# Attention with two expert layers on one core: a reordered opening, later casts, and weight decodes at other places

## The chip, the core and the metric

The kernel runs on one core of a Trainium2 chip. Its engines work from instruction queues of their own: TensorE (PE, matmuls, with its weight loads as PEld), VectorE (DVE), ScalarE (ACT), GpSimd (POOL) and SyncE (SP, which issues the DMAs here). The time is device microseconds of one execution, and the median of several is compared.

## What is computed

Attention over 2 batches of 8 heads with 768 positions of 64 numbers. Each query and each key is assigned to the nearest of 16 centroids of its head, and a query sees only keys of its own cluster. Two expert layers follow: the first with a leaky activation, the second behind an RMS norm with a SiLU gate.

```python
q_assign = argmax(einsum('bhsd,hcd->bhsc', q_n, c_n))      # q_n, k_n, c_n: unit vectors
k_assign = argmax(einsum('bhsd,hcd->bhsc', k_n, c_n))
scores = where(q_assign[..., None] == k_assign[..., None, :], q @ k.T / 8, -1e9)
attn = exp(scores - max(scores));  attn = attn / (sum(attn) + 1e-9)
x = reshape(attn @ v)                                      # 1536 tokens x 512
h = x @ w_in;  x = (max(h, 0) + alpha * min(h, 0)) @ w_out # 512 -> 2048 -> 512
xn = x / sqrt(mean(x * x) + 1e-6) * rms_g
out = (silu(xn @ w_gate) * (xn @ w_val)) @ w_out           # 512 -> 1536 -> 512
```

The expert weights arrive as 64-bit floats.

## The kernel before

**Attention** handles the 16 heads of both batches as 8 pairs. A pair has two phases of 384 queries, a phase has 6 slots, and a slot is one tile of 128 keys for both heads: `st_tile` multiplies it (L549 and L550 for each head), and ScalarE takes the exponential (L551). After every second slot `pv_tiles` multiplies with the values (L565) and sums the weights (L570). So there are 96 slots.

Each number of q and k is split in a high part, which is rounded (`prep_hi`, a ScalarE cast, L466, into a `stage` buffer), and a low part, the remainder (`prep_lo`, a subtraction on GpSimd, L471). Two operands per head, `op1` and `op2`, are put together from `stage` by DMAs that SP issues: `prep_dma_a` (L475, one copy) and `prep_dma_b` (L482 to L484, three). The clusters go into `op1` as 16 rows of one-hot code, built on chip and written by `prep_dma_oh` (L488), so that the mask falls out of the same matmul. The row maximum comes from `max_tile` a few slots ahead (two matmuls, L507, and one reduction over 768 columns on VectorE, L511); it is split (L516, L517) and turned into two rows of `op2` (`max_rows`, L534, L536).

The clusters of a pair need the vectors' norms. `prep_sq` squares on ScalarE (L367), `prep_ss` sums (L378: a tree on GpSimd for the pairs in `ASIDE`, 1 to 3), and `rnorm` makes three Newton steps (`prep_norm`; on VectorE L332 to L334, for `ASIDE` pairs on GpSimd L326 to L329). Then `prep_sims` multiplies with the centroids and transposes (L397, L402, L407), `prep_scale` scales (L414), `prep_arg` finds the nearest centroid (L423 to L436), and `prep_oht` turns the code round (L445, L446).

Three things set the order. `setup` writes the opening (pair 0 and the start of pair 1) by the letters of `CHAIN`, each of which takes the next step of one list: s and t sum squares of pairs 0 and 1, n Newton, l the loads of pair 1, m similarities, a scale and argmax, d the `prep_dma_a` copies, p the pattern (L294), o one-hot, q the squares of pair 1, w matmuls on zeros (L313) in the numbers of `WARM`. From then on `plan` places each step by (slot, order within the slot), from the tables `FIRST`, `SECOND`, `THIRD`, `FOURTH`, `FIFTH` and `PAIR` for pairs 0, 1, 2, 3, 4 and the rest, counted from the pair's first slot, and the maximum tiles from `AHEAD`. The inputs of a pair come into `nat` (for the norms) and `raw` (for the casts), two buffers of one name that each next pair takes over.

**The expert layers** (`Moe`) run 8 groups of the first layer and 6 of the second, each over three blocks of 512 tokens. `up` makes two halves of 128 hidden columns, and `down` two halves that are added into `x` (`down_mm`, then `down_add`, L914 on VectorE). Every product is three matmuls (`mm3`, L812): high by high, low by high, high by low. A group's weight halves are decoded on chip, one half a time: four instructions on VectorE (L788, L790, L793, L794), a ScalarE cast to the high part (L801), and two on GpSimd for the low part (L798, L799; on VectorE for those in `EAGER`). `plan` of `Moe` writes `up`, `down` and `decode_next` in a row: decodes go behind any half step with an open weight half, unless it is in `calm`. The RMS norm of a block is `rms_sq`, `rms_sum` (L933 to L942) and `rms_mul` (L950 to L958).

Of the kernel before, what the change touches and what calls it, by code (L numbers as in the profile page):

```python
# [47 lines left out]
FIFTH = {  # L48
    **PAIR,
    "load": ((-37, 6.1), (-37, 6.2), (-35, 1.8), (-35, 1.9)),  # L50
    "hi": ((-30, 4), (-29, 4)),
    "lo": ((-29, 4.5), (-28, 4.5)),
}
# [638 lines left out]
class Moe:  # L692
# [137 lines left out]
    def up_mm(self, i, n, c):  # L830
        self.ps[i, n, c] = ps = [self.bank(i)]
        if (i, n, c) in self.mid:
            self.proj(ps[0], i, "wi", n, c, (0, 1))
            self.rms_sum(self.mid[i, n, c])
            self.decode_next()
            self.proj(ps[0], i, "wi", n, c, (2, 3))
# [315 lines left out]
```

## Time and profile before

| | us |
|---|---|
| median of 3 runs (lowest to highest) | 907.59 (906.95 to 908.96) |
| the profiled execution | 905.67 |
| span of its trace | 903.9 |
| PE busy in it | 860.2 (95%) |
| DVE, POOL, ACT busy | 610.9, 395.8, 323.9 |

The span is what the trace covers, from the first instruction to the last; the profiled execution has 1.8 us around it. PE is busy nearly always, so the stretches in which it is not are looked at one by one. In the trace the opening is 0 to 33.2 us, the slots that follow run to about 320 us and later mix with the first expert groups, the first expert layer ends about 570 us, and the second ends the kernel.

### The profile page before, as it was taken

To read this page: it belongs to the slowest core of one execution; us is meant where nothing else is said; L and a number is where in the kernel's file an instruction comes from. 1 tells how busy PE (TensorE), PEld (TensorE's weight loads), DVE (VectorE), ACT (ScalarE), POOL (GpSimd) and SP (SyncE) were. 2 spreads that over 40 slices of the span, in tenths; PEclk is the share of its full clock that TensorE was granted. 3 is DMA by queue.
4 is the path that set the end of the run, shared out by engine and by line. 5 is a ranking of instruction groups with operands and counts; after the bars stand their busy time and mean duration, and the time that the engine had idled before them with its cause. 6 is when DMAs were issued, how large, how long until landed. Compare 5 with 4: busy or idle time off the path is not lost.

```text
span 903.9 us, 11594 instructions
## 1 busy us (share of the span) xinstructions
PE 860.2 (95%) x4358; PEld 636.6 (70%) x4358; DVE 610.9 (68%) x897; ACT 323.9 (36%) x623; POOL 395.8 (44%) x361
## 2 busy tenths in 40 slices
PE   6788999999999999999999989999999999999998
PEld 4455556555555678778887777877788888888886
DVE  7766775765467736887769897688995747383222
ACT  4345455554444524343342334443221212122110
POOL 5643220211001524666667677343784736374111
PEclk8699999999999999999999999999999999999999
DMA  6954474462371201221212222000331202020012
GB/s 195 213 157 119 130 166 114 124 154 56 100 185 49 89 21 39 69 80 61 75 52 94 70 94 71 1 24 26 115 106 58 87 30 94 24 70 1 1 41 99
DMA packets 24280, 75.69 MB, mean 84 GB/s; under 512 B 3681, under 2 KB 4897, under 8 KB 24225
## 3 DMA queue, kind: packets, MB, share of 16 engines
q1 hardware_dynamic: 24224, 74.96, 28.8%
q8 instruction: 34, 0.56, 0.3%
q14 instruction: 22, 0.17, 0.1%
HBM read 51.46 MB, written 3.15 MB: 60 GB/s over the span
## 4 chain that ended last, share of the span: by engine, by line
PE 69%; DVE 14%; ACT 6%; issue 4%; POOL 3%; DMA 2%; SPq 2%; ACTq 0%; POOLq 0%; DVEq 0%
PE ps_st L812 24%; PE ps_mx L812 10%; PE ps_pv L812 10%; PE ps_pv L565 6%; PE ps_pr L812 5%; PE ps_pv L570 3%; PE ps_mx L507 3%; DVE dec_a L790 3%; PE ps_st L549 3%; DVE x L914 2%; PE ps_st L550 2%; DVE dec_a L788 2%; DMA op<-stage 2%; ACT p L551 1%; DVE mx L511 1%
## 5 line engine op out<-in xcount | busy, mean ns | idle before, releaser
L511 DVE TENSOR_REDUCE mx<-ps_mx 128x1 f32<-128x768 f32 x93 | 88.9, 956 | 86.5 <-PE ps_mx L507 86.5
L872 POOL TENSOR_TENSOR gl<-v,gh 128x512 fp32r<-128x512 f32 x68 | 94.6, 1391 | 105.6 <-ACT gh L871 104.1
L551 ACT ACTIVATE p<-ps_st 128x384 f32<-128x384 f32 x192 | 83.1, 496 | 50.5 <-PE ps_st L550 50.1
L615 POOL TENSOR_TENSOR x1l<-X,x1h 128x384 fp32r<-128x384 f32 x15 | 15.1, 1008 | 163.9 <-ACT x1h L612 163.9
L812 PE MATMUL ps_st<-x1h,stage 128*128 128x512 f32 x272 | 84.3, 391 | 0.0
L790 DVE SCALAR_TENSOR_TENSOR dec_a<-raw,dec_a 128x512 uint32<-128x512 uint32 x66 | 81.7, 1238 | 2.3
L549 PE MATMUL ps_st<-op 128*128 128x384 f32 x192 | 71.7, 374 | 11.8 <-ACT p L551 11.8
L871 ACT CAST gh<-v 128x512 fp32r<-128x512 f32 x68 | 42.3, 622 | 112.0 <-DVE v L868 64.1
L868 DVE TENSOR_TENSOR v<-ps_st,t 128x512 f32<-128x512 f32 x36 | 24.9, 690 | 77.1 <-PE ps_st L812 76.9
L864 DVE SCALAR_TENSOR_TENSOR v<-v,alpha,t 128x512 f32<-128x512 f32 x45 | 43.9, 974 | 43.9 <-ACT v L863 43.9
L565 PE MATMUL ps_pv<-p,vnat 128*64 128x384 f32 x384 | 73.2, 502 | 0.0
L550 PE MATMUL ps_st<-op 82*128 82x384 f32 x192 | 65.5, 341 | 0.0
L798 POOL TENSOR_TENSOR dec_a<-dec_a,woh 128x512 f32<-128x512 f32 x27 | 42.9, 1589 | 45.1 <-ACT woh L801 42.1
L507 PE MATMUL ps_mx<-op 80*128 80x384 f32 x186 | 54.1, 372 | 6.1 <-DVE mx L511 6.1
L812 PEld LDWEIGHTS ps_st<-x1h,stage 128*128 128x128 f32 x272 | 50.9, 188 | 11.0
L812 PE MATMUL ps_st<-x1h,wvh 128*128 128x512 f32 x144 | 57.0, 396 | 0.9 <-ACT t L867 0.9
L914 DVE TENSOR_TENSOR x<-ps_mx,x 128x1024 f32<-128x1024 f32 x36 | 43.8, 1217 | 19.5 <-PE ps_mx L812 19.5
L812 PE MATMUL ps_st<-x1h,wvl 128*128 128x512 f32 x144 | 56.9, 395 | 0.0
L812 PE MATMUL ps_st<-x1l,wvh 128*128 128x512 f32 x144 | 56.8, 395 | 0.0
L914 DVE TENSOR_TENSOR x<-ps_pv,x 128x1024 f32<-128x1024 f32 x35 | 42.6, 1218 | 20.5 <-PE ps_pv L812 20.5
L507 PEld LDWEIGHTS ps_mx<-op 80*128 80x128 f32 x186 | 31.5, 193 | 34.6 <-issue 11.9
L549 PEld LDWEIGHTS ps_st<-op 128*128 128x128 f32 x192 | 36.6, 190 | 25.7 <-ACT p L551 24.1
(251 smaller groups left out, 2098.9 us busy)
## 6 DMA issues: line engine op xcount, KB each, us to landing
raw<-in_moe_w_out_dram SPq DMA_DIRECT2D x28, 512.0 KB, 3.5
op<-stage SPq DMA_DIRECT2D x32, 384.0 KB, 5.5
raw<-in_moe_w_in_dram SPq DMA_DIRECT2D x15, 512.0 KB, 3.6
raw<-in_moe_w_val_dram SPq DMA_DIRECT2D x12, 512.0 KB, 3.4
raw<-in_moe_w_gate_dram SPq DMA_DIRECT2D x12, 512.0 KB, 3.4
op<-stage SPq DMA_DIRECT2D x16, 288.0 KB, 5.8
nat<-in_qn_dram SPq DMA_DIRECT2D x8, 384.0 KB, 4.4
nat<-in_kn_dram SPq DMA_DIRECT2D x8, 384.0 KB, 5.2
```

The source lines that it names most:

```text
L507: nc.tensor.matmul(ps[:, g, :self.HS], lhsT=o1[0:80, 0, t * 128:(t + 1) * 128], rhs=o1[0:80, 1, sl], start=True, stop=True)
L511: nc.vector.tensor_reduce(out=self.mx[ph][:, k:k + 1], in_=ps[:, :, :self.HS], op=ALU.max, axis=AX.XY)
L549: nc.tensor.matmul(ps, lhsT=o1[:, 1, ks], rhs=o1[:, 0, qs], start=True, stop=False)
L550: nc.tensor.matmul(ps, lhsT=o2[:, 1, ks], rhs=o2[:, 0, qs], start=False, stop=True)
L551: nc.scalar.activation(out=p[:, e], in_=ps, func=AF.Exp, scale=self.scale)
L565: nc.tensor.matmul(ps[64 * e:64 * e + 64], lhsT=self.vnat[ph // 2][:, e, t0 + y], rhs=P[y][:, e], start=t0 + y == 0, stop=t0 + y == T - 1)
L790: v.scalar_tensor_tensor(out=a, in0=top, scalar=0xC0000000, in1=a, op0=ALU.bitwise_and, op1=ALU.bitwise_or)
L798: eng.tensor_tensor(out=af, in0=af, in1=f(hi), op=ALU.subtract)
L812: self.nc.tensor.matmul(ps, lhsT=a, rhs=b, start=first and i == 0, stop=last and i == len(terms) - 1)
L864: nc.vector.scalar_tensor_tensor(out=v, in0=v, scalar=self.nalpha[:, a], in1=t, op0=ALU.mult, op1=ALU.add)
L872: nc.gpsimd.tensor_tensor(out=lo, in0=v, in1=f(hi), op=ALU.subtract)
L914: nc.vector.tensor_tensor(out=dst, in0=ps, in1=dst, op=ALU.add)
```

## The change

1. **Buffers.** `nat` and `raw` become two each, by the parity of the pair, so that a pair's loads need not wait for the pair before.
2. **Opening.** `prep_lo` of pair 0 (a new letter v) goes from GpSimd to VectorE, behind the pattern; the squares of pair 1 go behind the one-hot step; 21 warm matmuls stand where 28 did.
3. **Pair 1.** Its Newton steps go from GpSimd to VectorE (9 instructions for 12). The one-hot copies of heads 2 and 3 stand in slot 4 ahead of their six `prep_dma_b` copies, which were placed in slots -1 and 0 and now are in 4 and 5.
4. **Tables.** Casts of later pairs one slot later and their low parts 4 to 9 slots later; loads earlier; `FIFTH` is gone. Where two maximum tiles fall in one slot, the second goes behind the slot's score matmuls.
5. **Experts.** Decodes go behind the first half (y = 0) of a step alone; (8, wo, 1) leaves `EAGER`; `rms_mul` of blocks 1 and 2 goes between a `down_mm` and its `down_add`; `rms_sum` in the middle of an `up` goes behind three of four column blocks; `mm3` puts all high-by-low products last.

```diff
 PAIR
-    "hi": ((-33, 4), (-32, 4)),
-    "lo": ((-32, 4.5), (-31, 4.5)),
+    "hi": ((-32, 4), (-31, 4)),
+    "lo": ((-28, 4.5), (-22, 4.5)),
...
 THIRD
-    "load": ((-30, 13), (-30, 13.1), (-26, 6), (-26, 6.1)),
+    "load": ((-36, 1.1), (-36, 1.2), (-36, 1.3), (-36, 1.4)),
...
-WARM = (6, 12, 5, 1, 4)
+WARM = (6, 10, 1, 1, 3)
-EAGER = ((0, "wi", 0), (0, "wi", 1), (1, "wi", 0), (8, "wo", 1))
+EAGER = ((0, "wi", 0), (0, "wi", 1), (1, "wi", 0))
 CALM = (0, 1)
+LATE = (1,2)
-CHAIN = "cccwccbbccccclcsscncncncnmnnnnmnnwnnnndllxlaaaxaqaawxpowqowtt"
+CHAIN = "cccwccbbccccclcsscncncncnmnnnnmnnwnnnndllxlaaaxaaawxpvvowowqqtt"
...
         for i in range(2):
             self.prep_hi(0, i)
-            self.prep_lo(0, i)
...
+            "v": [lambda i=i: self.prep_lo(0, i) for i in range(2)],
...
-            self.nat[pr] = self.pre([128, 2, self.T, 2, self.D], "nat")
+            self.nat[pr] = self.pre([128, 2, self.T, 2, self.D], f"nat{pr % 2}")
-            self.raw[pr] = self.pre([128, 2, self.S], "raw")
+            self.raw[pr] = self.pre([128, 2, self.S], f"raw{pr % 2}")
...
-            self.norm[pr] = self.rnorm(self.ss.pop(pr), [128, X, 2, 4], f"n{pr % 2}", pr in ASIDE)
+            self.norm[pr] = self.rnorm(self.ss.pop(pr), [128, X, 2, 4], f"n{pr % 2}", pr in ASIDE[1:])
...
-        nc.gpsimd.tensor_tensor(out=st[:, 2 - i], in0=self.raw[pr][:, i], in1=f(st[:, 3 * i]), op=ALU.subtract)
+        eng = nc.gpsimd if pr else nc.vector
+        eng.tensor_tensor(out=st[:, 2 - i], in0=self.raw[pr][:, i], in1=f(st[:, 3 * i]), op=ALU.subtract)
...
-                at(-1, 12, self.prep_dma_b, h)
-                at(0, 12, self.prep_dma_b, h + 1)
-                at(5, 0, self.prep_dma_oh, h)
-                at(5, 0, self.prep_dma_oh, h + 1)
+                at(4, 2.8, self.prep_dma_oh, h)
+                at(4, 2.8, self.prep_dma_oh, h + 1)
+                at(4, 12, self.prep_dma_b, h)
+                at(5, 12, self.prep_dma_b, h + 1)
...
-                at(s, 0.5 if s % 2 or s < 0 else 1.5, self.max_tile, ph, k)
+                at(s, 2.7 if s in slots[:k] else 0.5 if s % 2 or s < 0 else 1.5, self.max_tile, ph, k)
...
-        terms = []
-        for (ah, al), (bh, bl) in pairs:
-            terms += [(ah, bh), (al, bh), (ah, bl)]
+        terms = [t for (ah, al), (bh, bl) in pairs for t in ((ah, bh), (al, bh))]
+        terms += [(ah, bl) for (ah, al), (bh, bl) in pairs]
...
         self.down_mm(i, n, y)
+        if (i, n, y) in self.mul_at:
+            self.rms_mul(self.mul_at[i, n, y])
         self.down_add(i, n, y)
...
-                        calm |= {(self.up, *nxt[1], z) for z in CALM}
+                        calm |= {(self.up, *nxt[1], z) for z in CALM if n or z}
...
-                if todo and not busy:
+                if todo and not busy and y == 0:
                     dec.append(todo.pop(0))
                     out.append((self.decode_next,))
```

On VectorE in the opening, behind the scaling of pair 0's similarities (`code`, `am`, `oh` are steps of the argmax, `pat` the pattern, `mx` the maxima), there stands before:

```order
L428 TENSOR_TENSOR sims<-sims,code 128x384
L423 TENSOR_REDUCE am_282<-sims 128x24
L436 TENSOR_TENSOR oh<-code,am_282 128x3x16x2 x4
L294 ISA pat,ohs<-pat,idf 128x128
L294 ISA ohs 128x1
L511 TENSOR_REDUCE mx<-ps_mx 128x1
L511 TENSOR_REDUCE mx<-ps_pv 128x1
```

and now:

```order
L423 TENSOR_TENSOR sims<-sims,code 128x384
L418 TENSOR_REDUCE am_277<-sims 128x24
L431 TENSOR_TENSOR oh<-code,am_277 128x3x16x2 x4
L288 ISA pat,ohs<-pat,idf 128x128
L288 ISA ohs 128x1
L467 TENSOR_TENSOR stage_112<-raw_144,stage_112 128x768 x2
L507 TENSOR_REDUCE mx<-ps_mx 128x1
L507 TENSOR_REDUCE mx<-ps_pv 128x1
```

The two subtractions of `prep_lo` (now L467) have come in between the pattern and the first maximum.

On SP around the start of the slots (the number behind op1 or op2 names the head's buffer, 2 and 3 are the second pair's) there stands before:

```order
L482 DMA op1_2_123<-stage1_113 48x1536
L483 DMA op2_2_127<-stage1_113 64x1536
L484 DMA op2_2_127<-stage1_113 16x1536
L482 DMA op1_3_124<-stage1_113 48x1536
L483 DMA op2_3_128<-stage1_113 64x1536
L484 DMA op2_3_128<-stage1_113 16x1536
L1071 DMA alpha_62<-in_moe_alpha_dram 128x16
L1072 DMA rg_63<-in_moe2_rms_g_dram 128x4
L363 DMA vnat_540<-in_vn_dram 128x768
L357 DMA nat_606<-in_qn_dram 128x768
L357 DMA nat_606<-in_kn_dram 128x768
L488 DMA op1_2_123<-oht_598 16x4x384
```

and now:

```order
L352 DMA nat1_424<-in_kn_dram 128x768
L1074 DMA alpha_62<-in_moe_alpha_dram 128x16
L1075 DMA rg_63<-in_moe2_rms_g_dram 128x4
L358 DMA vnat_513<-in_vn_dram 128x768
L484 DMA op1_2_123<-oht_576 16x4x384
L484 DMA op1_3_124<-oht_576 16x4x384
L478 DMA op1_2_123<-stage1_113 48x1536
L479 DMA op2_2_127<-stage1_113 64x1536
L480 DMA op2_2_127<-stage1_113 16x1536
L478 DMA op1_3_124<-stage1_113 48x1536
L479 DMA op2_3_128<-stage1_113 64x1536
L480 DMA op2_3_128<-stage1_113 16x1536
```

The one-hot copies (`oht`) have passed the six copies from `stage1`, and the loads of `nat` stand ahead of them or behind them, no longer in between.

On VectorE in the first expert layer (v0 to v2 are activations, `x2_` the sums that `down_add` adds to, `dec_` a decode) there stands before:

```order
L864 SCALAR_TENSOR_TENSOR v2_3169<-v2_3169,alpha_62,t2_3168 128x512
L914 TENSOR_TENSOR x2_2_3165<-ps_mx_4579,x2_2_3165 128x1024
L914 TENSOR_TENSOR x2_2_3165<-ps_pv_4593,x2_2_3165 128x1024
L788 TENSOR_SCALAR dec_a0_2739<-raw_4529 128x512
L790 SCALAR_TENSOR_TENSOR dec_a0_2739<-raw_4529,dec_a0_2739 128x512
L793 TENSOR_SCALAR dec_e0_2740<-dec_a0_2739 128x512
L794 SCALAR_TENSOR_TENSOR dec_e0_2740<-raw_4529,dec_e0_2740 128x512
L864 SCALAR_TENSOR_TENSOR v0_2748<-v0_2748,alpha_62,t0_2747 128x512
L788 TENSOR_SCALAR dec_a1_2741<-raw_4556 128x512
L790 SCALAR_TENSOR_TENSOR dec_a1_2741<-raw_4556,dec_a1_2741 128x512
```

and now:

```order
L862 SCALAR_TENSOR_TENSOR v2_3159<-v2_3159,alpha_62,t2_3158 128x512
L914 TENSOR_TENSOR x2_2_3155<-ps_mx_4551,x2_2_3155 128x1024
L784 TENSOR_SCALAR dec_a0_2729<-raw_4487 128x512
L786 SCALAR_TENSOR_TENSOR dec_a0_2729<-raw_4487,dec_a0_2729 128x512
L789 TENSOR_SCALAR dec_e0_2730<-dec_a0_2729 128x512
L790 SCALAR_TENSOR_TENSOR dec_e0_2730<-raw_4487,dec_e0_2730 128x512
L914 TENSOR_TENSOR x2_2_3155<-ps_pv_4574,x2_2_3155 128x1024
L862 SCALAR_TENSOR_TENSOR v0_2738<-v0_2738,alpha_62,t0_2737 128x512
L784 TENSOR_SCALAR dec_a1_2731<-raw_4528 128x512
L786 SCALAR_TENSOR_TENSOR dec_a1_2731<-raw_4528,dec_a1_2731 128x512
```

The decode stood behind both additions of a `down` and now stands between them.

## Rows read from the trace of the kernel before

**Rows 1.** Busy us by stretch: length, PE, PEld, DVE, ACT, POOL, clock, DMA share.

```profile
0.00:33.20 33.20, 22.44 (x97) 14.49 (x98) 23.66 (x60) 12.52 (x19) 18.52 (x62) 0.81 0.68 188
33.20:57.00 23.80, 19.82 (x108) 10.82 (x108) 16.65 (x28) 11.20 (x22) 15.37 (x32) 0.84 0.96 247
57.00:320.00 263.00, 246.89 (x1659) 150.07 (x1659) 172.88 (x325) 129.76 (x291) 56.74 (x61) 1.00 0.45 115
320.00:480.00 160.00, 158.55 (x700) 128.60 (x697) 115.46 (x130) 57.38 (x103) 92.06 (x64) 1.00 0.16 54
480.00:560.00 80.00, 74.52 (x320) 59.19 (x319) 70.91 (x77) 28.76 (x52) 57.77 (x39) 1.00 0.26 88
560.00:640.00 80.00, 77.54 (x355) 62.27 (x354) 64.34 (x110) 32.67 (x51) 33.28 (x24) 1.00 0.09 29
640.00:903.80 263.80, 260.41 (x1130) 211.14 (x1128) 147.05 (x169) 51.59 (x87) 122.05 (x84) 1.00 0.17 58
```

**Rows 2.** Timeline of POOL in the opening: start us, duration us, instruction, idle before.

```profile
8.38 3.62 POOL L471 TENSOR_TENSOR stage<-raw,stage 128x768 fp32r<-128x768 f32 x2 [1.64 <-DMA raw<-in_kt_dram]
```

**Rows 3.** Timeline of DVE in the opening.

```profile
7.78 0.18 DVE L332 TENSOR_TENSOR n_a<-n_y,ss 128x24 f32<-128x24 f32 x1
8.43 1.80 DVE L332 TENSOR_TENSOR n_a<-n_y,ss 128x24 f32<-128x24 f32 x1
...
14.91 0.56 DVE L414 TENSOR_TENSOR sims<-ps_st,n_a 128x384 f32<-128x384 f32 x1
...
23.46 0.96 DVE L511 TENSOR_REDUCE mx<-ps_mx 128x1 f32<-128x768 f32 x1 [4.55 <-PE ps_mx L507]
```

**Rows 4.** Timeline of PE in the opening.

```profile
10.53 0.27 PE L407 MATMUL ps_st<-idf,simc 128*128 128x128 f32 x1
...
33.21 0.52 PE L549 MATMUL ps_st<-op 128*128 128x384 f32 x1
```

**Rows 5.** Timeline of ACT in the opening.

```profile
20.99 0.84 ACT L367 ACTIVATE nat<-nat 128x768 f32<-128x768 f32 x1
21.74 0.56 ACT L446 ACTIVATE oht<-ps_pr,ohs 128x384 fp32r<-128x384 f32 x1
```

**Rows 6.** Timeline of SP's queue: first and last copy issued before the first score tile.

```profile
22.33 0.63 SPq L488 DMA_DIRECT2D op<-oht  x1
...
28.34 1.70 SPq L484 DMA_DIRECT2D op<-stage  x1
```

**Rows 7.** DMA issues at 28.3 us: KB each, us to landing.

```profile
op<-stage SPq DMA_DIRECT2D x1, 96.0 KB, 5.4
```

**Rows 8.** Waits of ACT from 33.2 to 57: us in total, times, longest.

```profile
ACT stage L466 <- DMA raw<-in_kt_dram: 2.9, 1, 2.9
```

**Rows 9.** Timeline of PE, first maximum tile of the second pair.

```profile
56.87 0.62 PE L507 MATMUL ps_mx<-op 80*128 80x384 f32 x2
```

**Rows 10.** Waits of PE from 57 to 125.

```profile
PE ps_mx L507 <- DVE mx L511: 4.2, 4, 1.1
```

**Rows 11.** Waits of PE from 125 to 320.

```profile
PE ps_st L549 <- ACT p L551: 8.7, 26, 0.7
```

**Rows 12.** Waits of PE from 480 to 560.

```profile
PE ps_mx L812 <- DVE x L914: 3.4, 2, 2.8
```

**Rows 13.** Timeline of PE: starts of two `down` steps there.

```profile
533.63 0.47 PE L812 MATMUL ps_mx<-gh,woh 128*128 128x512 f32 x1 [2.79 <-DVE x L914]
...
545.94 0.48 PE L812 MATMUL ps_mx<-gh,woh 128*128 128x512 f32 x1 [1.11 <-ACT t L862]
```

**Rows 14.** Timeline of DVE: one instruction in two decodes there.

```profile
527.83 1.66 DVE L790 SCALAR_TENSOR_TENSOR dec_a<-raw,dec_a 128x512 uint32<-128x512 uint32 x1
...
535.05 0.69 DVE L790 SCALAR_TENSOR_TENSOR dec_a<-raw,dec_a 128x512 uint32<-128x512 uint32 x1
```

**Rows 15.** Timelines of DVE and POOL: first and last instruction of one decode.

```profile
377.49 1.52 DVE L788 TENSOR_SCALAR dec_a<-raw 128x512 uint32<-128x512 uint32 x1
...
383.13 1.38 POOL L799 TENSOR_TENSOR wil<-dec_a,dec_e 128x512 fp32r<-128x512 f32 x1
```

More of the change, by code (lines that the diff above doesn't have):

```diff
@@ L36 @@
     **PAIR,
-    "load": ((-32, 6.1), (-32, 6.2), (-28, 6.1), (-28, 6.2)),
+    "load": ((-38, 6.1), (-38, 6.2), (-30, 6.1), (-30, 6.2)),
     "sq": ((-30, 4), (-29, 4)),
@@ L47 @@
 }
[L48 to L53, printed above, removed]
 THIRD = {
     **PAIR,
-    "load": ((-30, 13), (-30, 13.1), (-26, 6), (-26, 6.1)),
-    "sq": ((-25, 4), (-24, 4)),
-    "ss": ((-24, 5), (-23, 5)),
-    "norm": tuple((-23 + n // 5, 5.1 + (n % 5) / 10) for n in range(17)),
+    "load": ((-36, 1.1), (-36, 1.2), (-36, 1.3), (-36, 1.4)),
+    "sq": ((-24, 4), (-23, 4)),
+    "ss": ((-23, 5), (-22, 5)),
+    "norm": tuple((-21 + n // 6, 5.1 + (n % 6) / 10) for n in range(17)),
     "hi": ((-23, 4), (-22, 4)),
@@ L62 @@
     "sims": ((-20, 1.7), (-19, 1.7)),
-    "scale": ((-19, 5),),
+    "scale": ((-18, 1.2),),
     "arg": ((-17, 5), (-16, 5), (-15, 5), (-15, 5.1), (-14, 5)),
@@ L68 @@
 SECOND = {
-    "hi": ((-18, 2.5), (-20, 0.3)),
-    "lo": ((-18, 10), (-19, 8)),
+    "hi": ((-18, 2.5), (-18, 2.6)),
+    "lo": ((-10, 4.5), (-9, 4.5)),
     "sims": ((-19, 8), (-16, 1.5)),
-    "norm": tuple((-18, 9 + n / 100) for n in range(14)) + tuple((-12, 5 + n / 100) for n in range(3)),
-    "scale": ((-12, 5.1),),
-    "arg": ((-11, 5.1), (-10, 5), (-10, 5.1), (-9, 5), (-9, 5.1)),
+    "norm": tuple((-18, 9 + n / 100) for n in range(14)),
+    "scale": ((-13, 5),),
+    "arg": ((-12, 5), (-11, 5), (-10, 5), (-10, 5.1), (-9, 5)),
     "oht": ((-8, 2.6),),
@@ L83 @@
     0: (-12, -11, -10, -9, -8, -7),
-    1: (-1, 0, 1, 2, 3, 4),
+    1: (0, 1, 2, 2, 3, 4),
     2: (7, 7, 8, 9, 9, 10),
-    3: (11, 12, 12, 13, 14, 15),
+    3: (11, 11, 12, 13, 14, 15),
 }
@@ L490, in early_load @@
     def early_load(self, x):
-        t = self.pre([128, 2, self.T, 2, self.D], "nat") if x == 0 else self.pre([128, 2, self.S], "raw")
+        t = self.pre([128, 2, self.T, 2, self.D], "nat0") if x == 0 else self.pre([128, 2, self.S], "raw0")
         t = (t.rearrange("p a t h d -> p (a t h d)") if x == 0 else t.rearrange("p a s -> p (a s)")).bitcast(U32)
@@ L628, in plan @@
             b = SLOTS * pr
-            tab = (FIRST, SECOND, THIRD, FOURTH, FIFTH, PAIR)[min(pr, 5)]
+            tab = (FIRST, SECOND, THIRD, FOURTH, PAIR)[min(pr, 4)]
             for key, fn in (("load", self.load), ("sq", self.prep_sq), ("ss", self.prep_ss), ("hi", self.prep_hi),
@@ L832, in up_mm @@
         if (i, n, c) in self.mid:
[L833 to L836, printed above, removed]
+            m = self.mid[i, n, c]
+            part = {1: 3, 2: 3}[m]
+            self.proj(ps[0], i, "wi", n, c, range(part))
+            self.rms_sum(m)
+            if m < self.NB - 1:
+                self.decode_next()
+            self.proj(ps[0], i, "wi", n, c, range(part, self.K))
         else:
@@ L981, in plan @@
         pre = len(dec)
-        rms_at, self.mid, calm = {}, {}, set()
+        rms_at, self.mid, self.mul_at, calm = {}, {}, {}, set()
         for fn, (i, n) in seq:
@@ L997, in plan @@
                             self.mid[(*nxt[1], 1)] = n
-                        rms_at[self.up, *nxt[1], 1] = (self.rms_mul, n)
-                        calm |= {(self.up, *nxt[1], z) for z in CALM}
+                        calm |= {(self.up, *nxt[1], z) for z in CALM if n or z}
+                        if n in LATE:
+                            self.mul_at[(n1 - 1, NB - 1, 0) if n < NB - 1 else (n1, 0, 0)] = n
+                        else:
+                            rms_at[self.up, *nxt[1], 1] = (self.rms_mul, n)
                 if last and y and fn == self.up:
@@ L1008, in plan @@
                         or (fn, i, n, y) in calm)
-                if (i, n, y) in self.mid and fn == self.up:
+                if self.mid.get((i, n, y), NB) < NB - 1 and fn == self.up:
                     dec.append(todo.pop(0))
-                if todo and not busy:
+                if todo and not busy and y == 0:
                     dec.append(todo.pop(0))
```

## The prediction

> **What bounds the kernel now.** I read the busy time by stretch first [rows 1]. PE is busy 860 of 903.9 us, so a change can win only where PE idles or runs below full clock. From 640 us on it idles 3.4 us of 263.8, from 320 to 480 us 1.5 of 160: nothing to speak of. The rest is in four places: the opening up to 33.2 us, in which PE's 22.4 us are mostly warm-up and the end is set by others; the first seven slots, 33.2 to 57 (4.0 idle, clock 0.84); the slots to 320 us (16.1 idle); and 480 to 640 us in the first expert layer (5.5 and 2.5 idle). For each of these I then read what the waiting engine waited for.
>
> *Opening.* GpSimd makes two subtractions of 128x768 from 8.38 to 12.00 [rows 2]. In that time VectorE's small Newton steps take ten times as long: the same instruction takes 0.18 at 7.78 and 1.80 at 8.43 [rows 3]. PE has the transposed similarities ready at 10.53 + 0.27 = 10.80 [rows 4], but VectorE scales them only at 14.91. The argmax, the one-hot code (ACT at 21.74, right behind a square of pair 1 [rows 5]) and its copy at 22.33 follow in a row. Six `prep_dma_b` copies are queued behind that copy, the last issued at 28.34 [rows 6]; such a copy takes 5.4 us to land [rows 7], 33.7, which is when the first score tile runs (33.21, its second head a little later) [rows 4]. So the chain is Newton, argmax, one-hot, copies, first score.
>
> *First slots.* The DMA share is 0.96 [rows 1]; ScalarE waits 2.9 us for one load of `raw` [rows 8], with exponentials queued behind it. The first maximum tile of pair 1 comes at 56.87 [rows 9].
>
> *Later slots.* From 57 to 125 PE waits four times for a maximum, 4.2 us in all [rows 10]: those are places where two maximum tiles stand back to back on one PSUM buffer and the second waits for the first's reduction. From 125 to 320 it waits 8.7 us for exponentials, in 26 small pieces [rows 11].
>
> *Experts.* From 480 to 560 VectorE is busy 70.9 of 80 us [rows 1]; PE waits there for `down_add` twice, 3.4 us in all [rows 12].
>
> **The change part by part**, against the profiled execution of 905.67 us, which is 1.92 under the median of 907.59; I carry that difference through.
>
> *Low parts of pair 0 to VectorE; squares of pair 1 behind.* Without GpSimd's two subtractions the nine small steps from 8.43 take about 0.2 to 0.3 each, so they end near 10.6, and scaling starts when PE is done, 10.8: 4.1 us earlier. The one-hot step no longer stands behind the 0.84 us square: 0.7 more. The copy chain could start 4.8 earlier. The subtractions themselves cost two times 128x768 on VectorE; the nearest clean row is 0.69 for a two-input instruction of 128x512 [rows 14], so about 1.03 each, 2.1 in all, behind the pattern, where VectorE idled 4.55 us ahead of the first maximum at 23.46 [rows 3]: hidden. Were that cover gone, the copies that carry low parts and the first maximum would be 2.1 later. I take **-4.5**. Bounds: -3 (the copies are then paced by their own landing, or a part of the 2.1 shows) and -6 (-4.8, and the last issue takes 0.63 instead of 1.70 [rows 6]).
>
> *Fewer warm matmuls.* PE waits anyway; the cost can only be through the clock, in the next term.
>
> *Buffers by parity, pair 1's Newton steps on VectorE, one-hot copies first.* The loads of pair 2 no longer wait for pair 1 to be squared and cast, so the 2.9 wait of ScalarE [rows 8] should go, and with it its exponentials' delay. The Newton steps are 9 instructions of some 0.2 to 0.3, 2.5 us, on a VectorE that is busy 16.7 of 23.8 [rows 1]: hidden, and the hops between two engines go. The one-hot copies make SP wait for ACT's one-hot code in slot 4, with six copies and the later loads queued behind; those serve the score tiles of slot 12, some 20 us later. In return the maxima of slot 7 need not wait for six other copies. Recoverable are at most the 4.0 us in which PE idles; I take **-3**. Bounds -4 and +2.4: a mean clock of 0.84 is one third of the stretch at 1.2 GHz and two thirds at 2.4; half and half would be 0.75, and 19.8 us of work would become 19.8 x 0.84 / 0.75 = 22.2.
>
> *Doubled maximum tiles taken apart.* The score matmuls now fill the time of the reduction (0.96 [rows 3]). Of 4.2 [rows 10] I take **-3.2**, as one of the four waits may be for a reduction that other work on VectorE delays. Bounds -1 and -4.2.
>
> *Later casts, low parts 4 to 9 slots later, loads earlier.* ScalarE is busy 130 of 263 us, GpSimd 57 [rows 1], and each result is wanted ten slots or more later: hidden. They are off the exponentials' way only in part; of 8.7 [rows 11] I take **-0.5**, bounds -2 and +1.
>
> *Decodes at other places.* From 480 to 560 a pair of steps (one `up`, one `down`) takes 545.94 - 533.63 = 12.31 us, of which 1.11 is waiting [rows 13]; 80 us hold 6.5 such pairs. Two halves are decoded in each pair before and after, so VectorE has the same work; I expect no gain there. The waits of 320 to 480 and 560 to 640 (1.5 + 2.5 = 3.9 [rows 1]) are single places where a decode stands ahead of something urgent; I take 3.2 of them, as some of it is a wait for a decoded half itself: **-3.2**. Bounds: -7.3 (all 3.9 and the 3.4 of [rows 12]) and +1. A decode now delays the second `down_add` by its 2 to 4 us; the bank that this addition frees is written next one pair of steps later, so PE has some 8 us in hand. `rms_mul` ahead of `down_add` is covered by the same; without that cover it would be some 1 us, twice. The order within `mm3` is the same matmuls: 0.
>
> **Sum.** -4.5 - 3 - 3.2 - 0.5 - 3.2 = -14.4: 905.67 becomes 891.3, and the median 907.59 becomes 893.2.
>
> **The rivals.**
>
> *A. Transfers pace the start.* The DMA share of 0.96 [rows 1] speaks for it: if bytes rather than waits set the first slots, the opening gives 3 and the slots nothing. -3 - 3.2 - 0.5 - 3.2 = -9.9: 897.7. Against it: ScalarE's waits there are for loads that were issued late.
>
> *B. VectorE becomes the bound in the first expert layer.* Of two neighbouring decodes one runs clean and one beside GpSimd: the same instruction takes 0.69 at 535.05 and 1.66 at 527.83 [rows 14], 0.97 more, and I take its neighbour of the same size as losing the same. Spread out, both decodes of a pair of steps may run beside GpSimd's work for the activations: 1.94 more per pair. VectorE idles 9.1 us in 80, 1.4 a pair, so about half shows: 7 x 0.97 = 6.8 us, 900.0. For it: VectorE is busy 89% there. Against it: with its work spread evenly no `down_add` stands behind two decodes.
>
> The Trainium skill ("SBUF — State Buffer", section "Who interferes with whom") has a rule for this: a VectorE instruction with two SBUF inputs and a GpSimd instruction that reads SBUF exclude each other, and the one issued first holds the ports to its end. The rows agree in direction, but 0.97 is less than a whole GpSimd instruction of 1.38 [rows 15]. By the rule each contended pair could lose a whole one, 7 x 1.38 = 9.7 us instead of 6.8, and B would come out at 902.9; I hold that for the smaller part of B.
>
> *C. Nearly all waits go.* -4.5 - 4 - 4.2 - 2 - 7.3 = -22: 885.6. For it: each of these waits is touched by the change. Against it: [rows 12], where VectorE has as much to do as before.
>
> *D. Slower: weight halves come too late in the second layer.* There a group has six halves to decode, and with decodes only behind first halves there are six places in its three blocks: no slack. A decode takes from 377.49 to 383.13 + 1.38, 7.0 us [rows 15]; the last half must be there two half steps (12.31 - 1.11 = 11.2 us [rows 13]) after its place. It decides from a decode of over 11.2 us. At twice the row, 14.0, each of the six groups would wait 2.8: +16.8, 910.0. Against it: 7.0 leaves 4 us.
>
> *E. The change does not show.* The chain at the start may have a second one just behind it (loads of pair 1, the first maxima), with the expert layers as before: 907.6. Against it: the 4.1 us at 8.43 have no other cause in the trace.
>
> **How the numbers follow.** Forecast 0.44, A 0.17, B 0.17, C 0.12, D 0.06, E 0.04. The time is the forecast's, 893. The forecast's own range is 889 to 897. The range 885 to 902 takes in A, C's milder half and most of B, and leaves out D, E, the upper end of B and what lies below 885, some 0.2 in all. A measurement of this kernel tells 0.2% (1.8 us) from no change. Forecast, A, B and C are faster: 0.90, of which I move 0.02 of B, with late halves on top, to the other two. Faster 0.88, same 0.05, slower 0.07.
>
> **What would show it.** Right: Newton steps of 0.2 us throughout and scaling at about 10.9; the first score tile near 29; the first maximum of pair 1 seven and a half us earlier than 56.87; no wait for a maximum of 1 us from then to the end of the next two pairs; 480 to 560 with the same pace of 12.3 us for a pair of steps. Wrong: subtractions on VectorE that themselves run long and push the first maximum (opening under 3); a first score tile that waits for the last copy with the queue full (A); the clean decode at 1.66 instead of 0.69 and a pair of steps of 13 us (B), or 11.2 (C); PE waiting for a decoded weight half from 640 us on, where it now idles 3.4 us (D).

## The result and the profile after

| | before | after |
|---|---|---|
| median of 4 runs (lowest to highest), us | 908.28 (906.95 to 909.05) | 894.83 (892.14 to 896.74) |
| the profiled execution (its span) | 905.67 (903.9) | 896.74 (895.0) |

The ratio is 0.9838 with an interval of 0.9807 to 0.9869: 13.5 us faster, where 14.4 was forecast. The profiled execution of after is the slowest of its four, and that of before is faster than the four of its median, so the two traces are only 8.9 us apart. Medians of before in the later comparisons lie between 907.6 and 910.3, those of the changed kernel at 894.8 and 896.0.

The stretches of after, as in [rows 1] (length, PE, PEld, DVE, ACT, POOL, clock, DMA share):

```profile
0.00:27.70 27.70, 20.18 (x87) 12.28 (x88) 21.83 (x69) 11.35 (x18) 11.22 (x51) 0.88 0.77 213
27.70:52.30 24.60, 20.32 (x113) 12.12 (x112) 15.49 (x31) 12.52 (x25) 15.59 (x28) 0.86 0.65 176
52.30:109.10 56.80, 51.95 (x335) 31.81 (x333) 38.50 (x81) 26.68 (x58) 15.85 (x29) 0.94 0.55 143
...
396.50:548.00 151.50, 150.57 (x651) 121.88 (x649) 131.03 (x141) 56.96 (x101) 109.38 (x71) 1.00 0.22 77
548.00:560.00 12.00, 7.88 (x24) 5.92 (x25) 6.36 (x8) 6.49 (x11) 6.99 (x5) 0.72 0.13 44
```

The opening is 5.5 us shorter. From 52 to 109 the mean clock is 0.94, where before it was full. From 396.5 to 548 PE idles 0.9 us, and then 4.1 of 12.

The opening answers to [rows 3, 4]. Timelines of DVE and of PE in after:

```profile
8.72 0.18 DVE L327 TENSOR_TENSOR n_a<-n_y,ss 128x24 f32<-128x24 f32 x1
...
12.15 0.56 DVE L409 TENSOR_TENSOR sims<-ps_st,n_a 128x384 f32<-128x384 f32 x1 [1.31 <-PE ps_st L402]
...
16.06 1.82 DVE L467 TENSOR_TENSOR stage<-raw,stage 128x768 fp32r<-128x768 f32 x2
```

```profile
27.76 0.42 PE L545 MATMUL ps_st<-op 128*128 128x384 f32 x1
...
30.05 0.41 PE L546 MATMUL ps_st<-op 82*128 82x384 f32 x1 [1.51 <-DMA op<-stage]
...
51.86 0.62 PE L503 MATMUL ps_mx<-op 80*128 80x384 f32 x2
52.32 0.34 PE L545 MATMUL ps_st<-op 128*128 128x384 f32 x1
```

PE in before, from the last wait ahead of the first score tile to slot 7 (L549 at 58.99):

```profile
30.59 0.58 PE L534 MATMUL ps_st<-idr,mh 128*64 128x128 f32 x3 [0.68 <-DVE mh L517]
...
34.11 0.33 PE L550 MATMUL ps_st<-op 82*128 82x384 f32 x1
...
58.53 0.62 PE L507 MATMUL ps_mx<-op 80*128 80x384 f32 x2 [1.05 <-DVE mx L511]
58.99 0.34 PE L549 MATMUL ps_st<-op 128*128 128x384 f32 x1
```

The Newton steps take 0.18 throughout, the two subtractions 1.82 instead of the estimated 2.1, and the first score tile starts at 27.76 instead of 33.21. Its second head now waits 1.51 us for the last copy, so that head gains less, 4.1 us (34.11 to 30.05). The slots behind it run at half clock in part (0.86), as before (0.84). The first maximum tile of pair 1 starts at 51.86 instead of 56.87, 5.0 us earlier, where the prediction has seven and a half.

The waits of PE from 52 to 120 us (in all, times, longest), for [rows 10]:

```profile
PE ps_mx L503 <- DVE mx L507: 2.6, 6, 1.1
PE ps_st L545 <- ACT p L547: 0.8, 3, 0.4
```

In the first expert layer the waits of [rows 12, 13] are gone, and one stands at its end. Timeline of PE:

```profile
552.06 0.80 PE L807 MATMUL ps_mx<-gh,woh 128*128 128x512 f32 x1 [4.46 <-ACT gh L869]
```

### The profile page after: what moved, and what is told of

It reads as the page before. It is cut to its first block, busy times and chain, and to the rows that moved or that the text cites. A ratio compares the mean times of both kernels' runs of the same rounds, so it can differ in the third digit from the quotient of the medians.

```text
span 895.0 us, 11602 instructions
## 1 busy us (share of the span) xinstructions
PE 861.4 (96%) x4351; PEld 639.6 (71%) x4351; DVE 586.1 (65%) x906; ACT 326.0 (36%) x623; POOL 393.6 (44%) x349
## 4 chain that ended last, share of the span: by engine, by line
PE 78%; DVE 10%; ACT 5%; issue 3%; POOL 1%; DMA 1%; SPq 1%; ACTq 0%; DVEq 0%
PE ps_st L807 26%; PE ps_mx L807 11%; PE ps_pv L807 10%; PE ps_pv L561 8%; PE ps_pr L807 5%; PE ps_pv L566 4%; PE ps_mx L503 4%; PE ps_st L545 3%; DVE dec_a L786 2%; PE ps_st L546 2%; PE ps_pr L594 2%; DVE x L914 1%; DVE dec_a L784 1%; ACT p L547 1%; ACT op L532 1%
## 5 line engine op out<-in xcount | busy, mean ns | idle before, releaser
L870 POOL TENSOR_TENSOR gl<-v,gh 128x512 fp32r<-128x512 f32 x68 | 93.7, 1378 | 110.3 <-ACT gh L869 108.5
L786 DVE SCALAR_TENSOR_TENSOR dec_a<-raw,dec_a 128x512 uint32<-128x512 uint32 x66 | 69.0, 1046 | 2.3
L862 DVE SCALAR_TENSOR_TENSOR v<-v,alpha,t 128x512 f32<-128x512 f32 x45 | 46.5, 1033 | 36.1 <-ACT v L861 36.1
L807 PE MATMUL ps_st<-x1h,stage 128*128 128x512 f32 x272 | 68.1, 391 | 0.0
L794 POOL TENSOR_TENSOR dec_a<-dec_a,woh 128x512 f32<-128x512 f32 x28 | 45.5, 1624 | 36.4 <-ACT woh L797 32.1
L807 PE MATMUL ps_st<-x1h,wih 128*128 128x512 f32 x132 | 52.7, 399 | 0.1
L807 PE MATMUL ps_st<-x1h,wil 128*128 128x512 f32 x132 | 51.9, 393 | 0.0
L789 DVE TENSOR_SCALAR dec_e<-dec_a 128x512 uint32<-128x512 uint32 x66 | 49.5, 750 | 2.2
```

Source lines behind the costliest of these rows:

```text
L786: v.scalar_tensor_tensor(out=a, in0=top, scalar=0xC0000000, in1=a, op0=ALU.bitwise_and, op1=ALU.bitwise_or)
L789: v.tensor_scalar(out=e, in0=a, scalar1=0xFF800000, scalar2=None, op0=ALU.bitwise_and)
L807: self.nc.tensor.matmul(ps, lhsT=a, rhs=b, start=first and i == 0, stop=last and i == len(terms) - 1)
L862: nc.vector.scalar_tensor_tensor(out=v, in0=v, scalar=self.nalpha[:, a], in1=t, op0=ALU.mult, op1=ALU.add)
L870: nc.gpsimd.tensor_tensor(out=lo, in0=v, in1=f(hi), op=ALU.subtract)
```

## The experiments

Each kernel is compared with before in several executions, and by one trace with the others. The table has, from the timelines of PE, the start of the first score matmul of some slots, of the 865th and 1057th expert matmul (both in the first layer, the second behind the long wait), and of the last matmul (us); r9 was timed once.

| | slot 0 | 7 | 15 | 24 | 56 | 865th | 1057th | last | median |
|---|---|---|---|---|---|---|---|---|---|
| before | 33.21 | 58.99 | 87.74 | 113.39 | 207.22 | 519.64 | 569.04 | 900.13 | 908.28 |
| after | 27.76 | 52.32 | 81.40 | 109.14 | 199.08 | 507.24 | 559.60 | 891.20 | 894.83 |
| r1, after again | 27.51 | 52.31 | 82.98 | 107.79 | 198.12 | 506.31 | 558.03 | 889.61 | 896.02 |
| r2, experts before | 27.82 | 51.09 | 80.17 | 104.98 | 194.89 | 507.43 | 556.80 | 887.89 | 895.71 |
| r3, opening before | 31.86 | 56.80 | 85.89 | 113.70 | 203.52 | 511.61 | 564.13 | 895.71 | 902.12 |
| r4, casts back | 27.84 | 51.80 | 80.87 | 109.49 | 202.54 | 510.63 | 563.65 | 895.26 | 901.58 |
| r5, low parts back | 27.31 | 51.60 | 80.68 | 108.40 | 199.08 | 507.17 | 560.82 | 892.32 | 896.37 |
| r6, maxima back | 27.66 | 54.96 | 83.70 | 108.52 | 199.22 | 507.29 | 559.82 | 891.34 | 898.34 |
| r10, pair 1 back | 28.17 | 56.03 | 87.71 | 112.52 | 202.41 | 510.62 | 562.50 | 894.09 | 899.15 |
| r9, quiet GpSimd | 28.10 | 52.26 | 81.34 | 106.16 | 196.22 | 504.36 | 548.76 | 880.27 | 885.81 |
| r7, values spread | 27.48 | 51.37 | 80.44 | 105.24 | 196.23 | 504.29 | 550.53 | 882.03 | 890.36 |
| r8, more warm matmuls | 28.90 | 53.93 | 83.02 | 107.83 | 198.52 | 506.60 | 559.53 | 891.06 | 897.01 |
| r11, rows sooner | 28.35 | 52.15 | 81.23 | 106.04 | 196.45 | 502.49 | 548.75 | 880.29 | 888.30 |
| r12, square sooner | 27.46 | 52.58 | 81.66 | 108.01 | 197.07 | 503.10 | 549.33 | 880.89 | 886.24 |

**r1: the changed kernel again.**

> The changed kernel once more, with nothing edited. Theory: in its profiled execution the clock fell to 1.2 GHz at 83 us (for some 7 us) and at 552 us, behind a wait of 4.46 us of TensorE in the first expert layer; the wait comes from the order of the work and stands in every execution, while the fall at 83 us does not, which makes the spread of 892.1 to 896.7. So: 892 to 897 us again, the wait at about 552 us within 0.5 us of 4.46. Rival: the wait is an accident of that execution too, and goes or has another size here.

896.02 (892.65 to 897.75). The wait at the end of the first layer is 4.46 us again; the fall of the clock at 83 us is absent, and one at 56 us has come. The theory holds: the wait belongs to the order of the work, the falls between 50 and 90 us do not.

**r3: the opening.** `CHAIN`, `WARM` and `prep_lo` as before.

```diff
-        eng = nc.gpsimd if pr else nc.vector
-        eng.tensor_tensor(out=st[:, 2 - i], ...
+        nc.gpsimd.tensor_tensor(out=st[:, 2 - i], ...
```

> The changed kernel with the opening of before (low parts of pair 0 on GpSimd right behind the casts, the old order of the letters, 28 warm matmuls). Theory: the Newton steps run long again beside GpSimd, the first score tile comes 5.4 us later, near 33.2 us, and nearly all of that stays to the end: 899 to 900 us. Rival: transfers pace the first slots, the later start is made up by the eighth slot, and the time is that of the changed kernel, 895 us.

902.12 (899.91 to 902.64), ratio to before 0.9926 (0.9904 to 0.9948): 6.1 us over r1. The long steps are back beside GpSimd's two subtractions (8.74 to 12.35). Timeline of DVE in r3:

```profile
8.93 1.68 DVE L329 SCALAR_TENSOR_TENSOR n_y<-n_a,n_y 128x24 f32<-128x24 f32 x1
10.64 1.74 DVE L327 TENSOR_TENSOR n_a<-n_y,ss 128x24 f32<-128x24 f32 x1
12.42 0.94 DVE L328 SCALAR_TENSOR_TENSOR n_a<-n_a,n_y 128x24 f32<-128x24 f32 x1
...
15.46 0.56 DVE L409 TENSOR_TENSOR sims<-ps_st,n_a 128x384 f32<-128x384 f32 x1
```

The scaling stands at 15.46, and in r1 at 11.60:

```profile
11.60 0.56 DVE L409 TENSOR_TENSOR sims<-ps_st,n_a 128x384 f32<-128x384 f32 x1 [0.72 <-PE ps_st L402]
```

So the new opening brings 3.9 us there. The first score tile starts 4.4 us later than in r1, not 5.4; the rest of the earlier start (33.21 to 31.86) is there with the old opening too, and no run says which edit it is owed to.

**r10: pair 1 as before.** `SECOND`, `ASIDE` and the places of its copies; the doubled buffers stay, and no run puts those back. The diff shows the main lines.

```diff
-                at(4, 2.8, self.prep_dma_oh, h)
...
-                at(4, 12, self.prep_dma_b, h)
...
+                at(-1, 12, self.prep_dma_b, h)
...
+                at(5, 0, self.prep_dma_oh, h)
...
-            ... pr in ASIDE[1:])
+            ... pr in ASIDE)
```

> The changed kernel with pair 1 treated as before: its Newton steps on GpSimd, its low parts early, its six copies in slots -1 and 0 and the one-hot copies behind them in slot 5. Theory: the opening alone carries most of the first 57 us; slots 0 to 7 (24.6 to 24.8 us in the changed kernel, 25.8 before) take 0.5 to 1.5 us longer, 897 us. Rival: the prediction's 3 us for this part, if the clock's falls hide it in the two traces: 899 us or more, slots 0 to 7 in 26 us or more.

899.15 (898.62 to 901.24), 3.1 us over r1. Slots 0 to 7 take 27.9 us (24.6 in after), and the first maximum of pair 1 waits for the late one-hot copy. Timeline of PE in r10:

```profile
55.57 0.44 PE L503 MATMUL ps_mx<-op 80*128 80x384 f32 x1 [1.68 <-DMA op<-oht]
```

The clock then falls for some 7 us. The numbers are the rival's, and the sign is clear: no execution of r10 is under 898.62, and none of the eight of after and r1 is over 897.75. The size is less so, since the ratios to before, each with medians of its own, overlap: 0.9881 (0.9841 to 0.9921) for r10, 0.9864 (0.9826 to 0.9903) for r1.

But r10 prices the edit beside the new opening only. From the first score tile to the first maximum of pair 1, r10 takes 27.4 us. Before takes 23.7 (33.21 to 56.87), without a wait for the one-hot copy [rows 9]; after takes 24.1 (27.76 to 51.86), and r3, which has the old opening and the new pair 1, 24.5 (31.86 to 56.36). So with the old opening the old pair 1 was in time, and what r10 loses is what the earlier opening would lose without this edit. Slots 0 to 7 are 1.2 us shorter in after than in before, but that is another edit's: the second maximum tile, which waits 1.05 at 58.53 ahead of slot 7, now stands behind that slot's score matmuls.

**r8: warm matmuls.**

```diff
-WARMS = ((-4, 0.3, 2),)
+WARMS = tuple((s, 0.6, 2) for s in range(-11, -6)) + ((-4, 0.3, 4),)
```

> The changed kernel with 12 more matmuls on zeros, two behind each of five maximum tiles of the first pair and two more ahead of the first score tile. Theory: TensorE does little from 18 to 26 us and the granted clock goes to half for 16 us between 20 and 40 us, in which the first slots run; with more work ahead the clock stays up and the first eight slots take 2 to 4 us less: 892 to 894 us. Rival: the first slots are paced by the copies and by ScalarE, and the clock is half there for another reason: 896 us, or later by the 2 us of the added matmuls.

897.01 (894.46 to 897.46): the theory falls. The same stretches of r1 and then of r8 (columns as in [rows 1]):

```profile
20.00:31.00 11.00, 8.28 (x33) 4.61 (x31) 8.72 (x25) 4.38 (x9) 4.82 (x12) 0.69 0.92 217
31.00:40.00 9.00, 8.30 (x30) 4.40 (x30) 5.72 (x8) 4.50 (x8) 7.99 (x10) 0.62 0.97 254
```

```profile
20.00:31.00 11.00, 8.57 (x46) 5.69 (x46) 9.09 (x25) 5.41 (x9) 5.37 (x12) 1.00 0.76 159
31.00:40.00 9.00, 7.42 (x31) 5.10 (x31) 5.18 (x7) 4.54 (x8) 6.14 (x8) 0.62 0.94 263
```

By these rows r1 is at half clock for 13.7 of the 20 us (the expectation has 16) and r8 for 6.8. The clock does stay at 2.4 GHz up to 31 us, but the first score tile comes 1.4 us later, and then the clock falls all the same. Here half clock in the first slots is not bought off by work ahead of them: slots 0 to 7 take 25.0 us in r8 and 24.8 in r1.

**r6: the doubled maxima.**

```diff
-                at(s, 2.7 if s in slots[:k] else 0.5 if s % 2 ...
+                at(s, 0.5 if s % 2 ...
```

> The changed kernel with the second maximum tile of a slot back to back with the first. Theory: four waits of 1.05 us for a reduction between 50 and 90 us come back in place of the 0.34 us ones, +2.5 to +3.5 us, 899 us, if the clock stays up. Rival: the reductions are on VectorE's way anyhow and the wait is only moved: 896 us.

898.34, with one execution far above the others (896.64 to 905.34). The waits of PE from 52 to 108.5 us are those of [rows 10] again:

```profile
PE ps_mx L503 <- DVE mx L507: 4.2, 4, 1.1
```

Against 2.6 in after this is 1.6 us. At full clock, from slot 5 (48.71 in r6, 46.79 in r7) to slot 24, r6 takes 59.81 us and r7 58.45: 1.4 us. Ahead of slot 5 r6 loses another 1.7 (1.9 there, 0.2 at slot 0), of which the half clock, longer here, has a part that one trace does not tell.

**r4 and r5: casts and low parts of pairs 4 to 7**, each back alone.

```diff
-    "hi": ((-32, 4), (-31, 4)),
+    "hi": ((-33, 4), (-32, 4)),
```

```diff
-    "lo": ((-28, 4.5), (-22, 4.5)),
+    "lo": ((-31, 4.5), (-30, 4.5)),
```

> The changed kernel with only the casts of pairs 4 to 7 a slot earlier again, as before (slots -33 and -32 for -32 and -31); the low parts stay late. Theory: casts of 0.83 us stand between exponentials in slots 28, 40 and 52 and TensorE waits for the exponentials in the slot behind: 1.2 to 1.4 us for each of three or four pairs, +3.9 to +5 us, 899 us, to be seen slot by slot between 110 and 210 us. Rival: it was the low parts on GpSimd, which no longer hold VectorE there: then nothing changes, 895 us.

> The changed kernel with only the low parts of pairs 4 to 7 earlier again (slots -31 and -30 for -28 and -22, right behind the casts); the casts stay a slot later. Theory: nothing to see in TensorE's slots from 110 to 210 us, since nothing there waits for GpSimd or for the small steps that it slows; 896 us, as the changed kernel. Rival: the low parts hold VectorE's small steps (1.4 to 1.8 us in place of 0.18) and with them the argmax or a maximum, and a part of the 3.9 us is lost here too: 898 us or more.

r4 901.58 (896.26 to 905.31), 5.6 us over r1; r5 896.37, nothing. Slots 24 to 56 take 93.8 us before, 89.9 in after, 93.1 in r4 and 90.7 in r5 (90.3 in r1). The 3.9 us between before and after lie in three places, slots 29 and 30, 41 and 42, 53 and 54, with 1.4, 1.2 and 1.3; r4 loses 1.4, 1.0 and 0.8 in the same places (3.1 over the whole stretch). So it was the casts. At the first place, ScalarE and then PE in before:

```profile
128.88 0.84 ACT L466 CAST stage<-raw 128x768 fp32r<-128x768 f32 x1 [3.82 <-DMA vnat<-in_vn_dram]
129.62 0.86 ACT L551 ACTIVATE p<-ps_st 128x384 f32<-128x384 f32 x2
130.37 0.83 ACT L466 CAST stage<-raw 128x768 fp32r<-128x768 f32 x1
```

```profile
130.15 0.44 PE L549 MATMUL ps_st<-op 128*128 128x384 f32 x1 [0.66 <-ACT p L551]
```

The waits of PE in these slots, before, after and r4:

```profile
PE ps_st L549 <- ACT p L551: 5.5, 16, 0.7
```

```profile
PE ps_st L545 <- ACT p L547: 3.2, 10, 0.5
```

```profile
PE ps_st L545 <- ACT p L547: 4.8, 15, 0.6
```

r4 also loses 2.1 us at 86 us, where pair 4's casts, which in before had other places, hold the rows of the maxima. That part of its median is no part of what the change brought.

**r2: the expert part.** All of `Moe` and `EAGER` as before.

> The changed attention with the expert layers of before (their plan, the order of the three matmuls, the place of the norm). Theory: the new places of the decodes bring little, 0.8 us from the first expert group to the end in the trace, since VectorE's 12.2 us for a pair of steps stay and its lag is paid in one wait in place of six; about 896 us, with the waits of before (0.6, 1.0, 2.8, 1.1 us) back between 480 and 550 us. Rival: the expert part carries the 3.2 us of the prediction or more: 898 us or above.

895.71 (893.45 to 897.86) against 896.02: the theory holds, the expert part brings nothing that can be measured. The wait of 2.79 [rows 13] is back (521.42 in r2), and the one of 4.46 is not there. The table shows two sides that nearly cancel: from slot 56 to the 865th expert matmul the new order takes 308.2 us (after and r1) and the old one 312.5 (r2; before 312.4), 4.3 less; from there to the 1057th it takes 52.4 and 51.7 against 49.4, and behind that 0.5 more.

**r7: the value weights spread**, and **r9: GpSimd kept quiet.** In r7 the four value halves of groups 8 and 9 are decoded one in each of groups 2 to 5; r9 leaves out GpSimd's two steps of the decodes of groups 6 and 7.

```diff
-                    if i + 4 in split_v:
-                        todo += halves(i + 4, ["wv"])
+                    if 2 <= i < 6:
+                        todo.append((n1 + (i - 2) // 2, "wv", i % 2))
```

```diff
         def rest():
+            if i in (6, 7):
+                return
```

> The changed kernel with the four decoded halves of the value weights of groups 8 and 9, which stand in groups 4 and 5 (two each, ahead of all others), placed one each in groups 2, 3, 4 and 5. Theory: with two decodes in each of six pairs of steps VectorE needs 12.2 us for a pair and TensorE 11.0; the lag adds up and is paid in the wait of 4.46 us at 552 us, behind which the clock falls. With five decodes in three pairs it does not add up: the wait shrinks under 1 us, the clock stays at 2.4 GHz there, and the time falls by 5 to 7 us, to 889 to 891 us. Rival: the wait belongs to the end of the first layer (the step that waits for the last activations) and stays, or the lag comes up at another place: 895 us or more.

> The changed kernel without the two GpSimd steps of the weight decodes of groups 6 and 7 (their low parts are left as the groups before wrote them, so this leaves work out). The decodes on VectorE, their number and their places stay. Theory: it is GpSimd's work beside the decodes that makes a pair of steps 12.2 us on VectorE; without it the decode's first two instructions take 0.4 to 0.5 and 0.7 us in place of up to 1.5 and 1.66, a pair of steps costs VectorE 9 to 10 us, less than TensorE's 11.0, and the wait of 4.46 us at 552 us goes or falls under 1.5 us, the fall of the clock with it. Rival: two decodes in a pair of steps are too many by their number alone: the wait keeps at least 3 us.

r9 has no wait of PE at all from 480 to 570 us, with the same number of decodes in the same places. Its row for 480 to 560:

```profile
480.00:560.00 80.00, 80.00 (x352) 65.20 (x351) 68.49 (x91) 32.91 (x57) 31.90 (x22) 1.00 0.24 79
```

A pair of steps takes 10.8 us there (518.73 to 529.52 from one `down_add` to the next pair's), with VectorE idle for 0.8 of it. So it is GpSimd's work beside the decodes, not their number. r7 gives 890.36 (887.60 to 892.94), ratio 0.9782 (0.9743 to 0.9822), 5.7 us under r1, and the waits shrink to two. PE in r7, waits from 480 to 570:

```profile
PE ps_mx L807 <- ACT gh L869: 0.8, 1, 0.8
PE ps_mx L807 <- POOL gl L870: 0.8, 1, 0.8
```

The clock is full there. From the 865th to the 1057th matmul r7 takes 46.2 us, r9 44.4, r1 51.7, before 49.4.

**r11 and r12: what is left of the waits for exponentials.** r11 stands on top of r7, r12 on top of r11.

```diff
-                at(end + 1, 0.7, self.max_rows, ph, None)
+                at(end, 2.55, self.max_rows, ph, None)
```

```diff
-    "sq": ((-35, 4), (-34, 4)),
+    "sq": ((-35, 4), (-34, 1.1)),
```

> The kernel with the value weights spread, and one edit more: from the third pair on the three small matmuls that turn the maxima into rows go ahead of the maximum tile that stood before them. Theory: of the waits for exponentials that are left, one of 0.45 us in each phase comes from ScalarE's two copies of these rows, which stand between exponentials; begun 0.46 us sooner they are through in time: 11 times 0.45, 4 to 5 us, 886 us. Rival: the small matmuls then wait for the split of the maxima on VectorE, or the copies wait for another: no gain or a loss, 890 us or above.

> The kernel with the value weights spread and the rows sooner, and the second square of pairs 4 to 7 moved within its slot from behind the value matmuls to right behind the slot's exponentials. Theory: in the kernel before this one three waits of 0.96 us at 118, 152 and 186 us stand where ScalarE makes the two copies of the rows and then this square (0.84 us) ahead of four exponentials; with the square in ScalarE's idle time ahead, the three waits go: -2.9 us, 885 to 886 us. Rival: the square then waits for its load, or the wait moves to the next cast: no change, 888 us.

r11 gives 888.30 (884.52 to 889.30), ratio 0.9754 (0.9717 to 0.9791); r12 gives 886.24 (883.83 to 889.37), ratio 0.9760 (0.9728 to 0.9792). Waits of PE for exponentials from 100 to 305 us in r7 and in r11, and from 108 to 304 in r12:

```profile
PE ps_st L545 <- ACT p L547: 8.0, 23, 0.9
```

```profile
PE ps_st L545 <- ACT p L547: 5.0, 14, 1.0
```

```profile
PE ps_st L545 <- ACT p L547: 2.9, 12, 0.8
```

r11 misses its 4 to 5 us, since in three slots (28, 40, 52) the copies of the rows now run into a square and PE waits 0.96. r12 takes all three of these waits away. The 0.77 that it has is in slot 42, behind a cast; r7 waits there too (0.90) and r11 does not. The median cannot tell r11 and r12 apart. Both beat before and after.

## Why the prediction was right, and where it was not

The total, the sign and the range held, in part by luck: several terms were wrong, and their errors went in opposite directions. By the traces the parts come to some 11 us (5.0 for the first two together, 1.5, 3.9 and about 1); the rest of the 13.5 between the medians is not assigned to any of them.

- **Opening, -4.5.** Right in its mechanism (r3: the steps run long only beside GpSimd) and near in size: 3.9 at the scaling (r3 to r1), 4.1 at the second head of the first tile and 5.5 at its first, 6.1 in the medians. Two readings were off. The scaling starts at 12.15 and not at 10.8, since PE's similarities are ready later. And in before no copy held the first score tile: PE's last wait ahead of it is 0.68 at 30.59, for the split of a maximum; the copies are what it waits for in after.
- **First slots, -3: not there as a term of its own.** The wait of 2.9 for `raw` did go, and the DMA share fell from 0.96 [rows 1] to 0.65, but the way from the first score tile to the first maximum of pair 1 stayed at 24 us, and PE idles 4.3 us of these slots (24.60 - 20.32) where it idled 4.0 [rows 1]. The step that failed is the one that took 3 of PE's 4.0 us of idle time as recoverable, on top of the opening's gain: before did not wait for its one-hot copy, so the wait that putting it first was to remove was not there. The two edits together bring 5.0 at that maximum, not 7.5, and the second (about 3 by r10) keeps what the first has won. The second chain close behind the first, of which E spoke, is there. A's price for these slots, nothing, is what the trace of after shows, but not for A's reason: the lower DMA share brought no time. What paces these slots is open.
- **Maxima, -3.2: too much.** The waits that shrank were 4.2 to 2.6, not to 1; the score matmuls between two maxima cover 0.7 us of each wait of 1.05, and the wait at 81 us stays whole. The medians (r6 2.3 us over r1) do not settle more than that.
- **Later casts, -0.5: far too little.** Slots 24 to 56 became 3.9 us shorter, of which r4, with the casts alone put back, loses 3.1 again; its median has another wait in it. The step read the whole of [rows 11] as small pieces owed to the exponentials themselves, and did not look at what stood ahead of them on ScalarE: two casts of 0.83 in every twelve slots, behind which PE waited, three pairs long. The low parts, as said, were worth nothing (r5).
- **Experts, -3.2: nothing in the medians, about 1 in the traces.** The single waits did go, and those of 480 to 546 us with them but for 0.4, against the forecast of no gain there. But VectorE's pace stayed (526.96 to 539.13 from one `down_add` to the next pair's, 12.17 us), as the prediction said, and PE, with less in its way, ran ahead of it at 11 us a pair until nothing was left to run on. From a `down` on PE to its first `down_add` it was 3.0 us (462.86 to 465.85) and six pairs later 10.0 (529.18 to 539.13); the lag came due in one wait of 4.46, and the clock fell with it (548 to 560, 0.72). The step that failed is the one that took waits as priced one by one, while the resource behind all of them had no more room than before. Rival B named that resource, and its point that the clean decode would come to lie beside GpSimd's work was right:

Timelines of DVE and of POOL in after:

```profile
528.54 1.66 DVE L786 SCALAR_TENSOR_TENSOR dec_a<-raw,dec_a 128x512 uint32<-128x512 uint32 x1
...
533.10 1.52 DVE L784 TENSOR_SCALAR dec_a<-raw 128x512 uint32<-128x512 uint32 x1
534.66 1.66 DVE L786 SCALAR_TENSOR_TENSOR dec_a<-raw,dec_a 128x512 uint32<-128x512 uint32 x1
```

```profile
528.15 1.50 POOL L870 TENSOR_TENSOR gl<-v,gh 128x512 fp32r<-128x512 f32 x1
...
532.61 1.73 POOL L795 TENSOR_TENSOR wol<-dec_a,dec_e 128x512 fp32r<-128x512 f32 x1
534.30 1.47 POOL L870 TENSOR_TENSOR stage<-v,stage 128x512 fp32r<-128x512 f32 x1
```

Both decodes of a pair now have the long form (0.69 in [rows 14]). Each long instruction ends a little behind GpSimd's, and the two of one line by the same: 530.20 is 0.55 behind 529.65, 536.32 is 0.55 behind 535.77; that of the other line, 534.62, is 0.28 behind 534.34. So the trace reads as if VectorE stood still until GpSimd's instruction is nearly over. That is the rule of the Trainium skill ("SBUF — State Buffer", section "Who interferes with whom"), that the one issued first holds the shared ports to its end; the trace agrees, and r9 shows what it costs. The prediction's doubt of it, that 0.97 is less than a whole instruction of GpSimd, was wrong: at 528.54 the VectorE instruction starts 0.39 into GpSimd's 1.50, so only the rest could be lost.

D did not come: no wait for a weight half from 640 us on.

## What to carry to other kernels

A wait that vanishes is a gain only if the engine that caused it has room; add up that engine's busy time over the stretch, and expect the lag at the next place that cannot run ahead. Two engines of which one holds up the other should be read side by side, instruction by instruction, end against end. Where two terms of a sum lie on one path, price the second beside the first: a step that was in time can be late once the work ahead of it is earlier. And where many waits of one kind stand in a row, ask what was queued ahead of the instruction that is waited for: here the place of two casts of 0.8 us was worth 1.2 to 1.4 us in each of three places.

## What the runs showed of the clock

Two executions with the same order of work on every engine up to the experts differ here. The stretch from 80 to 92 us in after, and in r7 (columns as in [rows 1]):

```profile
80.00:92.00 12.00, 10.44 (x52) 6.93 (x53) 7.43 (x16) 3.85 (x9) 0.00 (x0) 0.72 0.52 160
```

```profile
80.00:92.00 12.00, 11.38 (x81) 6.77 (x82) 9.09 (x25) 5.54 (x12) 0.00 (x0) 1.00 0.46 143
```

In both, PE waits 1.05 and 0.62 us at the start of it; then the clock goes to 1.2 GHz for some 7 us in after and not in r7. What decides it is open. From slot 7 to 24 after takes 56.8 us, r7 53.9, so such a fall is worth some 3 us, as much as the edits that were to be told apart; a single trace says more between two falls than from start to end.
